# K of the first two tiles projected 256 columns wide, and one semaphore and one accumulating output DMA per block of 512 tokens

## Chip, cores, metric

One core of one Trainium2 chip. The metric is the device time of one execution in microseconds (us); the other cores are idle. For every run the record also holds the span of that execution, from the first to the last instruction, and the mean granted TensorE clock (0.999 or 1.000 in all runs told here). The difference of time and span, "time less span", I also call the fixed part. (Spans are recorded to 0.1 us, so a single difference carries up to 0.05 us of rounding.)

## The reference

A layer norm of x (2048 tokens of 640), then two branches added to x: attention of 32 heads of 20 over 8 keys at distance 0, 2, ... 14, and a gated linear unit of width 1536.

```python
x  = A_x                                  # [1, 2048, 640], bf16
xn = (x - mean(x)) / sqrt(var(x) + 1e-5)
q, k, v = split(xn @ wqkv)                # 32 heads of 20
logits = einsum("bhsd,bhswd->bhsw", q, k[pos - 2 * w]) * 20 ** -0.5   # w = 0..7, masked where pos - 2w < 0
o   = einsum("bhsw,bhswd->bhsd", softmax(logits), v[pos - 2 * w])
out = x + o @ wo + ((xn @ w_gate) * (xn @ w_up)) @ w_down
```

## The kernel before

A list of operations is built in program order; a small scheduler derives the semaphores. A DMA has a semaphore of its own and adds 16 to it; whoever depends on the DMA waits for 16.

```python
class Sched:
    def op(self, eng, fn, r=(), w=(), dma=False, name="", group=None):
        # ... dependencies X.deps from the bytes read (r) and written (w)
        if dma:
            X.event = (self.nc.alloc_semaphore(f"dma{self.n_dma}"), 16)
            self.n_dma += 1
    def emit(self, finals):
        # ... per operation: wait_ge for each dependency not known to be met; at the end:
        for X in finals:                       # the output DMAs
            prog["sp"].append((0,) + X.event)
```

The first two tiles of 128 tokens are projected tile by tile, as soon as their normalised rows are there. Five chunks c of the contraction are accumulated; five groups m of 128 output columns lie side by side in the 512-wide fp32 banks of PSUM (four of them in one bank, the fifth in the shared bank bm).

```python
    def proj_tile(which, tiles, bm, at={}):            # its matmul is line L496, 128 x 128
        for c, (t, b) in [(c, tb) for c in range(NCH) for tb in tiles]:
            col = (2 * which + t) * TS
            for m in range(NCH):
                # ... at[c, m]() puts the transposes of later tiles in between
                o = PS[:, b, m * TS:(m + 1) * TS] if m < 4 else PS[:, bm, col:col + TS]
                l, x = wcols(which, c, m), XNT[:, c, t * TS:(t + 1) * TS]
                # ... op("pe", matmul(o, l, x, start=..., stop=...))

    def proj_wide(which, t0, m, b, col):               # tiles 2 and 3: line L503, 128 x 256
        # ... five matmuls, two tiles at once

    bm = 1
    proj_tile(0, [(0, 0)], bm, {(4, 0): lambda: ln_pe(1, 0, 2), (4, 3): lambda: tr(1, 2)})   # Q of tile 0
    part_evac(0, 0, 1, 0, 4, 0, 0)
    proj_tile(0, [(1, 2)], bm)                                                              # Q of tile 1
    part_evac(0, 1, 1, 0, 4, 2, 0)
    ln_apply(3)
    proj_tile(1, [(0, 3), (1, 4)], bm, {(2, 0): lambda: tr(2), (3, 0): lambda: tr(3)})       # K of both
    ln_start(4)
    for t in (0, 1):
        part_evac(1, t, 1, 0, 4, 3 + t, 0)
    # ... then K and Q of tiles 2 and 3 (L503), V of tiles 0 to 3 (L476), the rest
```

The output of three blocks of 512 tokens is computed transposed: five groups of 17 matmuls per block (down_t, L667), each evicted by ScalarE into a slot of DT, turned by a DMA transpose into FACC, and added to the output in DRAM (which holds x by then) by an accumulating DMA from GpSimd. The last block comes untransposed (tail, L697): VectorE adds x from XR and the rows are stored.

```python
    def down_t(j, d):
        # ... 17 matmuls into bank b
        o = DT[:, (NCH * j + d) % 4]
        op("act", lambda e: e.activation(o, PS[:, b, :], ACT.Copy), r=[PS[:, b, :]], w=[o], name=f"fin{j}_{d}")
        f = FACC[j][:, :, cols]
        op("sp", lambda e: e.dma_start_transpose(f, o), r=[o], w=[f], dma=True, name=f"oT{j}_{d}")
        if d < NCH - 1:
            return
        for u in range(0, NJ, 2):
            f2 = FACC[j][:, u:u + 2]
            # ... h = 256 rows of the output
            stores.append(op("pool", ... e.dma_start(h, f2, accum_op=ALU.add), r=[f2, ("out",)], w=[("out", t)], dma=True))
```

## Time and profile before

| | before |
|---|---|
| time, median of the first 3 runs | 253.98 us (253.9 to 254.27) |
| span of the profiled run | 251.6 us (that run: 253.68 us) |
| TensorE busy | 98% of the span |
| chain that ended last | 96% TensorE |
| last wait for a load on the chain | Q weights, landed at 7.18 us |
| last addition on VectorE | starts at 249.33 us |

In the chain's pieces the columns are start, duration, engine and line, and the number of instructions merged. Dividing a piece's duration by its count gives the interval from one matmul to the next, which is what a stream of matmuls costs; the mean duration of one in the grouped view is two to four times as long, since neighbours overlap. The lines themselves stand in the prediction.

### The profile page before, as it was taken

To read this page: it belongs to the slowest core of one execution; us is meant where nothing else is said; L and a number is where in the kernel's file an instruction comes from. 1 tells how busy PE (TensorE), PEld (TensorE's weight loads), DVE (VectorE), ACT (ScalarE), POOL (GpSimd) and SP (SyncE) were. 2 spreads that over 40 slices of the span, in tenths; PEclk is the share of its full clock that TensorE was granted. 3 is DMA by queue.
4 is the path that set the end of the run, shared out by engine and by line. 5 is a ranking of instruction groups with operands and counts; after the bars stand their busy time and mean duration, and the time that the engine had idled before them with its cause. 6 is when DMAs were issued, how large, how long until landed. Compare 5 with 4: busy or idle time off the path is not lost.

```text
span 251.6 us, 3326 instructions
## 1 busy us (share of the span) xinstructions
PE 247.1 (98%) x1299; PEld 129.0 (51%) x1319; DVE 215.8 (86%) x255; ACT 114.6 (46%) x203; POOL 35.9 (14%) x44
## 2 busy tenths in 40 slices
PE   8999999999999999999999999999999999999996
PEld 3995555555544444444444444444444444445775
DVE  5899889999999953999999995999999999993221
ACT  5486657555555557555555554125555011111000
POOL 1000001044433231002331110003000000300300
DMA  6999679657678462355379931495300010581641
GB/s 188 311 263 204 123 204 407 161 105 125 117 135 138 72 125 42 122 215 104 63 130 270 517 95 28 44 341 88 50 3 0 21 42 21 65 125 24 115 115 52
DMA packets 33824, 33.78 MB, mean 134 GB/s; under 512 B 18033, under 2 KB 30321, under 8 KB 33777
## 3 DMA queue, kind: packets, MB, share of 16 engines
q1 hardware_dynamic: 27280, 24.13, 33.5%
q0 software_dynamic: 6240, 9.31, 22.8%
q8 instruction: 10, 0.16, 0.3%
q10 hardware_dynamic: 288, 0.13, 0.2%
q14 instruction: 6, 0.04, 0.1%
HBM read 14.42 MB, written 4.59 MB: 76 GB/s over the span
## 4 chain that ended last, share of the span: by engine, by line
PE 96%; DMA 1%; SPq 1%; issue 1%; DVE 0%
PE PS L642 41%; PE PS L667 22%; PE PS L476 21%; PE PS L697 7%; PE PS L503 2%; PE PS L496 2%; DMA WQKV<-in_A_wqkv_dram 1%; SPq L295 1%; PE PS L435 0%; DVE FOUT L701 0%
## 5 line engine op out<-in xcount | busy, mean ns | idle before, releaser
L642 PE MATMUL PS<-XNT,WU 128*128 128x512 bf16 x237 | 59.0, 379 | 0.2
L642 PE MATMUL PS<-XNT,WG 128*128 128x512 bf16 x232 | 57.9, 379 | 0.4
L476 PE MATMUL PS<-XNT,WQKV 128*128 128x512 bf16 x245 | 53.7, 379 | 0.3
L609 DVE TENSOR_TENSOR PVB<-VO,ATB 128x10240 f16<-128x10240 bf16 x8 | 43.9, 5488 | 0.2
L476 PEld LDWEIGHTS PS<-XNT,WQKV 128*128 128x128 bf16 x250 | 29.4, 118 | 24.4
L644 ACT ACTIVATE USX<-PS 128x512 bf16<-128x512 f32 x48 | 28.7, 597 | 22.6 <-PE PS L642 22.2
L642 PEld LDWEIGHTS PS<-XNT,WU 128*128 128x128 bf16 x240 | 23.5, 98 | 28.3
L642 PEld LDWEIGHTS PS<-XNT,WG 128*128 128x128 bf16 x240 | 23.5, 98 | 28.3
L604 DVE TENSOR_TENSOR PVB<-PVB 128x5120 f16<-128x5120 f16 (+1 forms) x16 | 34.5, 2155 | 0.3
L537 POOL DMA_DIRECT2D LOG<-PE x24 | 21.8, 910 | 55.5 <-DMA LOG<-PE 55.5
L644 ACT ACTIVATE HT<-PS 128x512 bf16<-128x512 f32 x36 | 21.5, 597 | 16.4 <-PE PS L642 16.4
L670 ACT ACTIVATE DT<-PS 128x512 f16<-128x512 f32 x15 | 9.0, 597 | 43.8 <-PE PS L667 40.7
L667 PE MATMUL PS<-HT,WD 128*128 128x512 bf16 x118 | 27.4, 379 | 0.1
L526 DVE TENSOR_TENSOR TMP<-QH,KH 128x2048 f16<-128x2048 bf16 x16 | 19.1, 1216 | 0.7 <-ACT KH L483 0.7
L667 PEld LDWEIGHTS PS<-HT,WD 128*128 128x128 bf16 x120 | 11.8, 98 | 14.1
L526 DVE TENSOR_TENSOR PP<-QH,KH 128x2048 f16<-128x2048 bf16 x16 | 18.9, 1217 | 0.0
L531 DVE TENSOR_TENSOR PP<-PP,TMP 128x4096 f16<-128x4096 f16 x8 | 18.3, 2291 | 0.2
L679 POOL DMA_DIRECT2D out_dram<-FACC x6 | 7.2, 1434 | 79.3 <-DMA FACC<-DT 79.3
L667 PE MATMUL PS<-VO,WO 128*128 128x512 bf16 x74 | 18.4, 379 | 0.0
L701 DVE TENSOR_TENSOR FOUT<-PS,XR 128x320 bf16<-128x320 f32 (+2 forms) x9 | 4.1, 454 | 16.6 <-PE PS L697 16.6
L537 POOL DMA_DIRECT2D PE<-PP x8 | 7.9, 985 | 64.7 <-DVE PP L532 64.7
L483 ACT ACTIVATE VO<-PS 128x512 bf16<-128x512 f32 x20 | 11.9, 596 | 8.6 <-PE PS L476 8.4
(69 smaller groups left out, 231.9 us busy)
## 6 DMA issues: line engine op xcount, KB each, us to landing
PE<-PP POOLq DMA_DIRECT2D x8, 512.0 KB, 4.7
ATB<-LOG SPq DMA_DIRECT2D x8, 512.0 KB, 4.5
LOG<-PE POOLq DMA_DIRECT2D x24, 128.0 KB, 2.7
WG<-in_B_w_gate_dram SPq DMA_DIRECT2D x1, 1920.0 KB, 8.0
WU<-in_B_w_up_dram SPq DMA_DIRECT2D x1, 1920.0 KB, 14.6
WD<-in_B_w_down_dram SPq DMA_DIRECT2D x1, 1920.0 KB, 10.2
out_dram<-in_A_x_dram SPq DMA_DIRECT2D x1, 1920.0 KB, 9.3
out_dram<-FACC POOLq DMA_DIRECT2D x6, 320.0 KB, 5.3
```

The lines of the kernel that those rows point to most:

```text
L476: op("pe", (lambda l, x, c: lambda e: e.matmul(PS[:, b, :], l, x, start=(c == 0), stop=(c == NCH - 1)))(l, x, c), r=[l, x], w=[PS[:, b, :] ...
L483: op("act", lambda e: e.activation(o, PS[:, b, :], ACT.Copy, scale=sc), r=[PS[:, b, :]], w=[o], name=f"pev{which}_{m}_{j}")
L526: return (1.22, lambda: op("dve", lambda e: e.tensor_tensor(o, qw, kw, ALU.mult), r=[q, k], w=[o], name=f"prod{h}_{p}_{c}"))
L531: (2.3, lambda: op("dve", lambda e: e.tensor_tensor(a, a, b, ALU.add), r=[a, b], w=[a], name=f"psum{h}_{p}")),
L537: op("pool", lambda e: e.dma_start(o, i, accum_op=ALU.add), r=[o, i], w=[o], dma=True, name=name)
L604: return lambda: op("dve", lambda e: e.tensor_tensor(o, x, y, ALU.add), r=[x, y], w=[o], name=f"{name}_{b}")
L609: lambda: op("dve", lambda e: e.tensor_tensor(PVB[:], vw, aw, ALU.mult), r=[v, a], w=[PVB[:]], name=f"pv_{b}")),
L642: op("pe", (lambda l, x, c: lambda e: e.matmul(PS[:, b, :], l, x, start=(c == 0), stop=(c == NCH - 1)))(l, x, c), r=[l, x], w=[PS[:, b, :] ...
L644: op("act", lambda e: e.activation(o, PS[:, b, :], ACT.Copy), r=[PS[:, b, :]], w=[o], name=f"guev{which}_{m}_{j}")
L667: op("pe", (lambda l, x, i: lambda e: e.matmul(PS[:, b, :], l, x, start=(i == 0), stop=(i == n - 1)))(l, x, i), r=[l, x], w=[PS[:, b, :]], ...
L670: op("act", lambda e: e.activation(o, PS[:, b, :], ACT.Copy), r=[PS[:, b, :]], w=[o], name=f"fin{j}_{d}")
L697: op("pe", (lambda l, x, i, b, wid: lambda e: e.matmul(PS[:, b, 0:wid], l, x, start=(i == 0), stop=(i == n - 1)))(l, x, i, b, wid), r=[l, ...
```

## The change

Its intent: fewer, wider matmuls at the start (25 of 256 columns for K of tiles 0 and 1 instead of 50 of 128); fewer semaphores, waits and DMAs at the output (five transposes count on one semaphore up to 80, DT has eight slots, one accumulating DMA of 640 KB takes the place of two of 320 KB).

```diff
--- before.py
+++ after.py
@@ -53,6 +53,10 @@
         self.pitch = {}
         self.clock = {e: nc.alloc_semaphore(f"clk_{e}") for e in ("act", "pe", "dve", "pool")}
         self.n_dma = 0
+
+    def dma_event(self, n):
+        self.n_dma += 1
+        return self.nc.alloc_semaphore(f"dma{self.n_dma - 1}"), 16 * n
 
     def sbuf(self, name, shape, dtype, offset):
         t = self.nc.alloc_sbuf_tensor_at(name, shape, dtype, offset=offset)
@@ -90,7 +94,7 @@
                 out.add(g)
         return [(g, q) for g in out for q in quads]
 
-    def op(self, eng, fn, r=(), w=(), dma=False, name="", group=None):
+    def op(self, eng, fn, r=(), w=(), dma=False, name="", group=None, event=None):
         X = _Op()
         X.eng, X.fn, X.name, X.dma = eng, fn, name, dma
         X.needs_tick, X.event, X.pre_know, X.idx = False, None, None, len(self.ops)
@@ -147,8 +151,7 @@
                 before = [] if st is None else st[0] + st[1]
                 self.state[k] = [[X], [], group, before]
         if dma:
-            X.event = (self.nc.alloc_semaphore(f"dma{self.n_dma}"), 16)
-            self.n_dma += 1
+            X.event = event or self.dma_event(1)
         self.ops.append(X)
         return X
 
@@ -272,7 +275,7 @@
     XR = sb("XR", [128, NXR, D])
     NFO = 4
     FOUT = sb("FOUT", [128, NFO, D])
-    DT = sb("DT", [128, 4, JB], FP16, at=K.base[ATB[1].name] + NSB * W * SB * 2)
+    DT = [sb(f"DT{k}", [128, 4, JB], FP16, at=K.base[ATB[k].name] + NSB * W * SB * 2) for k in range(2)]
     FACC = [sb(f"FACC{k}", [128, NJ, D], FP16, at=a) for k, a in
             enumerate((place[0] - NFO * D * 2, K.base[ATB[0].name], K.base[ATB[0].name] + NJ * D * 2))]
     NUS = 7
@@ -483,18 +486,15 @@
         op("act", lambda e: e.activation(o, PS[:, b, :], ACT.Copy, scale=sc), r=[PS[:, b, :]], w=[o],
            name=f"pev{which}_{m}_{j}")
 
-    def proj_tile(which, tiles, bm, at={}):
-        for c, (t, b) in [(c, tb) for c in range(NCH) for tb in tiles]:
-            col = (2 * which + t) * TS
-            for m in range(NCH):
-                if (c, m) in at and t == tiles[0][0]:
-                    at[c, m]()
-                o = PS[:, b, m * TS:(m + 1) * TS] if m < 4 else PS[:, bm, col:col + TS]
-                l, x = wcols(which, c, m), XNT[:, c, t * TS:(t + 1) * TS]
-                st = c == 0 and (m == 0 or m == 4 and t == tiles[0][0])
-                sp = c == NCH - 1 and (m == 3 or m == 4 and t == tiles[-1][0])
-                op("pe", (lambda o, l, x, st, sp: lambda e: e.matmul(o, l, x, start=st, stop=sp))(o, l, x, st, sp),
-                   r=[l, x], w=[o], name=f"pp{which}_{m}_{t}_{c}")
+    def proj_tile(which, t, b, bm, at={}):
+        for c, m in [(c, m) for c in range(NCH) for m in range(NCH)]:
+            if (c, m) in at:
+                at[c, m]()
+            o = PS[:, b, m * TS:(m + 1) * TS] if m < 4 else PS[:, bm, t * TS:(t + 1) * TS]
+            l, x = wcols(which, c, m), XNT[:, c, t * TS:(t + 1) * TS]
+            st, sp = c == 0 and m in (0, 4), c == NCH - 1 and m in (3, 4)
+            op("pe", (lambda o, l, x, st, sp: lambda e: e.matmul(o, l, x, start=st, stop=sp))(o, l, x, st, sp),
+               r=[l, x], w=[o], name=f"pp{which}_{m}_{t}_{c}")
 
     def proj_wide(which, t0, m, b, col):
         o = PS[:, b, col:col + 2 * TS]
@@ -654,6 +654,8 @@
 
     stores = []
 
+    t_event = [None]
+
     def down_t(j, d):
         flush_h(0)
         b = bank()
@@ -666,18 +668,20 @@
                 l, x = WO[:, i - NF, cols], VO[:, i - NF, toks]
             op("pe", (lambda l, x, i: lambda e: e.matmul(PS[:, b, :], l, x, start=(i == 0), stop=(i == n - 1)))(l, x, i),
                r=[l, x], w=[PS[:, b, :]], name=f"dt{j}_{d}_{i}")
-        o = DT[:, (NCH * j + d) % 4]
+        k = NCH * j + d
+        o = DT[k // 4 % 2][:, k % 4]
+        if d == 0:
+            t_event[0] = K.dma_event(NCH)
         op("act", lambda e: e.activation(o, PS[:, b, :], ACT.Copy), r=[PS[:, b, :]], w=[o], name=f"fin{j}_{d}")
         f = FACC[j][:, :, cols]
-        op("sp", lambda e: e.dma_start_transpose(f, o), r=[o], w=[f], dma=True, name=f"oT{j}_{d}")
+        op("sp", lambda e: e.dma_start_transpose(f, o), r=[o], w=[f], dma=True, name=f"oT{j}_{d}",
+           event=t_event[0])
         if d < NCH - 1:
             return
-        for u in range(0, NJ, 2):
-            f2 = FACC[j][:, u:u + 2]
-            t = NJ * j + u
-            h = ohbm[t * TS:(t + 2) * TS, :].rearrange("(u p) n -> p u n", p=TS)
-            stores.append(op("pool", (lambda h, f2: lambda e: e.dma_start(h, f2, accum_op=ALU.add))(h, f2), r=[f2, ("out",)],
-                             w=[("out", t)], dma=True, name=f"oacc{t}"))
+        acc = FACC[j][:]
+        h = ohbm[j * JB:(j + 1) * JB, :].rearrange("(u p) n -> p u n", p=TS)
+        stores.append(op("pool", lambda e: e.dma_start(h, acc, accum_op=ALU.add), r=[acc, ("out",)], w=[("out", j)], dma=True,
+                         name=f"oacc{j}"))
 
     def tail(t, nb):
         j, rows = t // 4, slice((t % 4) * TS, (t % 4 + 1) * TS)
@@ -758,15 +762,23 @@
             t_ln[0] += 1.45
 
     bm = 1
-    proj_tile(0, [(0, 0)], bm, {(4, 0): lambda: ln_pe(1, 0, 2), (4, 3): lambda: tr(1, 2)})
+    proj_tile(0, 0, 0, bm, {(4, 0): lambda: ln_pe(1, 0, 2), (4, 3): lambda: tr(1, 2)})
     part_evac(0, 0, 1, 0, 4, 0, 0)
-    proj_tile(0, [(1, 2)], bm)
+    proj_tile(0, 1, 2, bm)
     part_evac(0, 1, 1, 0, 4, 2, 0)
     ln_apply(3)
-    proj_tile(1, [(0, 3), (1, 4)], bm, {(2, 0): lambda: tr(2), (3, 0): lambda: tr(3)})
+    for c in range(NCH):
+        if c in (2, 3):
+            tr(c)
+        for m in range(NCH):
+            o = PS[:, bm, 2 * TS:] if m == 4 else PS[:, 3 + m // 2, m % 2 * 2 * TS:(m % 2 + 1) * 2 * TS]
+            l, x = wcols(1, c, m), XNT[:, c, 0:2 * TS]
+            st, sp = c == 0 and m % 2 == 0, c == NCH - 1 and m in (1, 3, 4)
+            op("pe", (lambda o, l, x, st, sp: lambda e: e.matmul(o, l, x, start=st, stop=sp))(o, l, x, st, sp),
+               r=[l, x], w=[o], name=f"pw1_{m}_0_{c}")
     ln_start(4)
-    for t in (0, 1):
-        part_evac(1, t, 1, 0, 4, 3 + t, 0)
+    for m in (0, 2):
+        part_evac(1, 0, 2, m, 2, 3 + m // 2, 0)
     ln_pace(12.0)
     for u in (0, 1):
         part_evac(u, 0, 2, 4, 1, bm, 2 * u * TS)
```

## The prediction

> **What bounds the kernel now.** I read the page's first part and its chain of waits, then the chain in order of time for the first 20 us (where the first part of the change lies), then the waits of the last 22 us and the DMA issues (where the second part ends).
>
> ```profile
> PE 247.1 (98%) x1299; PEld 129.0 (51%) x1319; DVE 215.8 (86%) x255; ACT 114.6 (46%) x203; POOL 35.9 (14%) x44
> ...
> PE 96%; DMA 1%; SPq 1%; issue 1%; DVE 0%
> ```
>
> TensorE is busy in 98% of the span and the chain that ended last is 96% TensorE. A busy share alone proves little, as the ends of matmuls are modelled, so I looked for gaps in the chain in order of time:
>
> ```profile
> 3.55 3.63 DMA WQKV<-in_A_wqkv_dram
> 7.18 0.05 issue
> 7.23 0.36 PE PS L496 x3
> 7.59 0.17 PE PS L435 x3
> 7.76 2.73 PE PS L496 x47
> 10.49 0.28 PE PS L435 x5
> 10.77 0.56 PE PS L496 x10
> 11.33 0.28 PE PS L435 x5
> 11.61 1.12 PE PS L496 x20
> 12.73 5.46 PE PS L503 x50
> 18.18 0.05 issue
> ```
>
> The last thing that is waited for on the path is a load of Q weights, landing at 7.18 us. From there to 249.3 us it is one stream of matmuls; the 0.05 us pieces of "issue" come once per about 49 matmuls and fit one record missing from the trace (49 pieces in 10.74 us plus 0.05 is 10.79, which is 50 times 216 ns), so I count them as no gap. The end is then: 7.2 us of start, the sum of the matmul intervals, the last addition on VectorE (249.33 for 0.29 us), and the last store. Only what alters the number or the interval of matmuls, or puts a wait into that stream, can move the time. L496 is the 128-wide projection (100 matmuls, Q and K of tiles 0 and 1), L503 the 256-wide one, L435 the transposes.
>
> The durations of single matmuls would mislead: the grouped view gives 220 ns for one at L496 and 273 ns at L503, but those contain the fill and drain that neighbours share. What counts is the interval, from the chain: 1.12 us / 20 = 56.0 ns, 0.56 / 10 = 56.0 ns, and 5.46 / 50 = 109.2 ns. (The piece of 47 reads 58.1 ns. It holds the start of Q of tile 1, where the issue rate drops for half a microsecond near 8.3 us, close to the end of ScalarE's copy of that tile; that is upstream of the change and stays.)
>
> For the output side, the waits of the last 22 us, then three lines of the waits of the whole span and three of the DMA issues:
>
> ```profile
> DVE FOUT L701 <- PE PS L697: 16.6, 9, 4.2
> POOL out_dram L679 <- DMA FACC<-DT: 14.4, 1, 14.4
> ACT DT L670 <- PE PS L667: 3.1, 1, 3.1
> ```
>
> ```profile
> POOL out_dram L679 <- DMA FACC<-DT: 79.3, 3, 42.8
> ...
> ACT DT L670 <- PE PS L667: 40.7, 14, 3.1
> ...
> ACT DT L670 <- remote: 3.1, 1, 3.1
> ```
>
> ```profile
> out_dram<-FACC POOLq DMA_DIRECT2D x6, 320.0 KB, 5.3
> XR<-in_A_x_dram SPq DMA_DIRECT2D x4, 160.0 KB, 7.7
> FACC<-DT SPq DMA_TRANSPOSE x15, 2.3
> ```
>
> GpSimd's 79 us are idle time of an engine with nothing else to do. The eviction into DT waits for TensorE and never, as far as the view shows, for its buffer: 14 of the 15 waits name TensorE, and the one put down to "remote" is 3.1 us, just as long as the others, so it too is the wait for 17 matmuls. No TensorE wait stands in these views after 7.2 us.
>
> **What the Trainium skill says.** "TensorE: Matmul & The Clock Gate", section "Wait — 56ns, not 53.3ns?", gives the start-to-start of back-to-back warm matmuls as N / 2.4 GHz plus about 2.5 ns: 55.8 ns for 128 and 109.2 ns for 256. The trace agrees to the digit (56.0 and 109.2). The same page, "Back-to-back issue gap", says that a stream of weight loads and matmuls sustains about 81 ns per matmul at N = 128; here the trace differs (56 ns with one weight load of 118 ns per matmul beside it), and the trace decides. That matters: with 81 ns the first part of the change would be worth 50 x 81 - 25 x 109 = 1.3 us. "DMA: Bandwidth & Descriptors", section "Why a DMA increments its semaphore by 16 and not by 1", says that with several DMAs on one semaphore only the full sum tells that all have landed. The change waits for 80 = 5 x 16, so it is sound, but whoever needs one transpose now waits for all five. The same page, "Anatomy of one DMA — SWDGE (gpsimd) path", fits 2.0 us plus bytes / 436 GB/s; that would be 2.75 us for 320 KB, and the trace shows 5.3, so I don't use it.
>
> **Part 1, K of tiles 0 and 1.** Removed: 50 matmuls of 128 columns (two tiles x 5 chunks x 5 column groups) with 50 weight loads. Added: 25 of 256 columns with 25 weight loads. The same columns go through the array, so only the fixed part of each interval is saved: 50 x 56.0 = 2.80 us against 25 x 109.2 = 2.73 us, a gain of 0.07 us (the skill's formula gives 25 x 2.5 ns = 0.06). The 25 weight loads saved are 25 x 118 ns = 2.95 us of the weight-load row, all beside matmuls: at 56 ns per matmul they plainly do not set the pace. All of the 0.07 us lies on the path, provided that no wait appears. Four could:
> - K weights. The five chunks are issued from 4.98 to about 7.3 us and land 3.7 to 4.2 us after issue, so at about 8.7 to 11.1 us. Chunk 0 is first used near 9.4 us, chunk 4 near 12.1. Slack 0.7 to 1 us, and the new order asks for them at most 0.07 us earlier.
> - Transposes of tiles 2 and 3 stay before chunks 2 and 3. VectorE finishes their inputs near 10.1 and 10.8 us; they run at 10.49 and 11.33 and would move up by 0.03 and 0.05 us.
> - The next 256-wide group needs ScalarE's copy of tile 3, over at 12.35 us, and starts near 12.6. The copy follows the transpose, which moves up as well, so the slack shrinks only by what the last ten matmuls save, 0.03 us.
> - Banks. The four K evictions (0.6 us each) become four of the same 512 columns, ready at the same place in the stream (about 0.3 us before its end); the banks are next used by V after 18 us, when they have long been read.
>
> **Part 2, transposes and output.** DT grows from four slots to eight and waits for a slot become waits for a whole block. Slot 0 is reused at the ninth eviction (second block, fourth), some 40 us after block 0's transposes landed: no wait. One 640 KB accumulating DMA replaces two of 320 KB per block, 6 issues become 3. GpSimd spends 2.39 to 2.42 us on a pair; I estimate 1.5 to 2.4 us for one, as the number of rows is the same. Nothing waits for GpSimd. The last block's pair is issued at 234.0 us and has landed by about 243; the program ends at 251.6. The final waits for stores become three fewer, but they stand in front of the wait for the last store (0.8 us), which hides them. Worth on the path: 0.
>
> Sum: 253.98 - 0.07 - 0 = 253.91 us.
>
> **Rivals.**
> (a) A wait takes the place of the saving: chunk 2 or the copy of tile 3 comes too late by a hair. For: slacks of 0.2 us, and in the half microsecond near 8.3 us TensorE did slow down beside such a copy. Against: everything that it waits for moves up too. It would return the 0.07 us, or add up to 0.1: 253.9 to 254.1.
> (b) The bigger output transfer delays the reload of XR for tile 14. For: that load, issued at 236.4 us, took 6.0 us against 2.7 for tile 15's, since it ran beside the two accumulating DMAs, and VectorE's addition for tile 14 starts at 242.41, 0.05 us late by the rhythm of 2.307 us (240.05 + 2.31 = 242.36). Against: if the one DMA starts 1.2 us later because all its descriptors are made first, and ends later by the same, VectorE makes it up in the idle 1.8 us before each following addition; eight banks let TensorE run on. Time unchanged, unless XR comes 7 us late.
> (c) The narrow matmuls are paced by weight loads, as the skill's 81 ns would have it, and halving them gains over a microsecond: 252.7. Against: 56 ns measured in this very stage.
> (d) Fewer semaphores and waits shorten the fixed part outside the span (253.7 of that profiled run against a span of 251.6). I see nothing in the views for it; up to some tenths, 253.6.
>
> **Range and chances.** 2% is 5.1 us; the largest thing I can build from these views is 1.3 us. The three runs before lie 0.37 us apart (253.9 to 254.27), five times the gain, so the width of the range is that of the measurement and of (a) and (d): 253.4 to 254.4. Within 2%: 0.98, 0.01 on either side.
>
> **What would show it.** In the changed profile: no line of 128-wide matmuls for K, 50 matmuls in the 128-wide group instead of 100, a new group of 25 of 256 columns with 109 ns intervals, and the 256-wide group of tiles 2 and 3 beginning 0.07 us earlier against the landing of the Q weights. Output: three issues of 640 KB, evictions still waiting for TensorE alone, XR of tile 14 landing between 5 and 8 us, the last addition and the last store in the same rhythm. I am wrong if a TensorE wait appears between 9 and 13 us or after 230 us, if the interval at 256 columns is not 109 ns there, or if the span falls by more than 0.3 us, which would mean a cost that these views do not show. The start (weights landing at 7.18 us) may vary between runs by more than the gain.

## The result, and the profile after

| | before | after |
|---|---|---|
| median, 6 runs each, same rounds | 254.06 us (253.65 to 254.29) | 253.64 us (253.39 to 254.07) |
| ratio, after over before | | 0.9987, 95% interval 0.9973 to 1.0001 |
| span of the profiled run | 251.6 us | 251.6 us |
| time less span | 2.08 us (27 runs of the later rounds, 2.03 to 2.13) | 1.79 us (6 runs, 1.77 to 1.81) |

A ratio here is the mean time of one kernel's runs over that of the other's of the same rounds, so not quite the ratio of the medians. The change is within 2%: faster by an estimated 0.33 us, with an interval from 0.03 us slower to 0.69 us faster, so that no difference is just not excluded.

The page of the kernel after, first line and summary of the chain:

```profile
PE 248.1 (99%) x1294; PEld 128.7 (51%) x1294; DVE 215.7 (86%) x255; ACT 114.6 (46%) x203; POOL 32.5 (13%) x41
...
PE 96%; DMA 1%; SPq 1%; issue 0%; DVE 0%
```

The bound is the same. TensorE's matmul and weight-load counts now agree (1294 each); in the trace of before 20 matmul records were missing. So the regular 0.05 us pieces of "issue" there were missing records, as the prediction took them to be: here the chain has no such piece after 18 us. Its pieces in order of time, whole from the landing of the Q weights to the end:

```profile
3.55 3.73 DMA WQKV<-in_A_wqkv_dram
7.28 0.05 issue
7.33 0.36 PE PS L496 x3
7.69 0.17 PE PS L438 x3
7.86 1.62 PE PS L496 x27
9.47 1.09 PE PS L777 x10
10.57 0.28 PE PS L438 x5
10.84 0.55 PE PS L777 x5
11.39 0.28 PE PS L438 x5
11.67 1.09 PE PS L777 x10
12.76 5.46 PE PS L503 x50
18.22 53.96 PE PS L479 x250
72.18 77.70 PE PS L642 x360
149.88 18.35 PE PS L669 x85
168.22 25.90 PE PS L642 x120
194.12 36.69 PE PS L669 x170
230.81 18.53 PE PS L701 x153
249.34 0.02 issue
249.37 0.29 DVE FOUT L705
```

L777 is the new group: 1.09 us for ten, 109 ns each. K with the two sets of transposes takes 12.76 - 9.47 = 3.29 us. Before, its first 20 matmuls are the 2.73 us of the piece of 47 less the 1.62 us that the 27 of Q take here, so 1.11; with 0.28, 0.56, 0.28 and 1.12 that makes 3.35 us. The 0.06 us is there. Counted from the landing of the Q weights, as the prediction asked, the 256-wide group of tiles 2 and 3 starts 0.07 us earlier (12.76 - 7.28 = 5.48 us against 12.73 - 7.18 = 5.55). The span does not show it, because the Q weights landed 0.10 us later in this run. From the start of the 256-wide group of tiles 2 and 3 to the last addition both traces read the same: 249.33 - 12.73 = 236.60 us before and 249.37 - 12.76 = 236.61 after. Not one of the changes to the output side moved TensorE's stream.

The output side, after: waits from 229 us to the end, and two lines of the DMA issues of the page and of its window from 230 us.

```profile
POOL out_dram L683 <- DMA FACC<-DT: 17.0, 1, 17.0
DVE FOUT L705 <- PE PS L701: 15.4, 9, 3.0
ACT DT L675 <- PE PS L669: 3.1, 1, 3.1
```

```profile
out_dram<-FACC POOLq DMA_DIRECT2D x3, 640.0 KB, 6.7
```

```profile
out_dram<-FACC POOLq DMA_DIRECT2D x1, 640.0 KB, 6.6
```

The same three waits as before, no new one. GpSimd's timeline, before and then after (start, duration, what, in brackets the idle time ahead of it):

```profile
234.03 2.39 POOL L679 DMA_DIRECT2D out_dram<-FACC  x2 [14.42 <-DMA FACC<-DT]
```

```profile
234.12 1.26 POOL L683 DMA_DIRECT2D out_dram<-FACC  x1 [17.04 <-DMA FACC<-DT]
```

One DMA of twice the size costs GpSimd about as much as one of the two did. The reload of XR for tile 14 took 5.4 us instead of 6.0, and the addition of tile 14 now starts in the rhythm of the others. The reload for tile 15 took 4.1 us instead of 2.7; its addition kept the rhythm too.

So where do some 0.3 us come from, if the span of the profiled run is the same? From the last row of the table: each run of the kernel after has a shorter time outside its span.

### The profile page after: what moved, and what is told of

The parts are those of the page before. It is cut to its first block, busy times and chain, and to the rows that moved or that the text cites. A ratio compares the mean times of both kernels' runs of the same rounds, so it can differ in the third digit from the quotient of the medians.

```text
span 251.6 us, 3277 instructions
## 1 busy us (share of the span) xinstructions
PE 248.1 (99%) x1294; PEld 128.7 (51%) x1294; DVE 215.7 (86%) x255; ACT 114.6 (46%) x203; POOL 32.5 (13%) x41
## 4 chain that ended last, share of the span: by engine, by line
PE 96%; DMA 1%; SPq 1%; issue 0%; DVE 0%
PE PS L642 41%; PE PS L669 22%; PE PS L479 21%; PE PS L701 7%; PE PS L503 2%; DMA WQKV<-in_A_wqkv_dram 1%; PE PS L777 1%; SPq L298 1%; PE PS L496 1%; PE PS L438 0%; DVE FOUT L705 0%
## 5 line engine op out<-in xcount | busy, mean ns | idle before, releaser
L642 PE MATMUL PS<-XNT,WU 128*128 128x512 bf16 x240 | 59.6, 379 | 0.0
L642 PE MATMUL PS<-XNT,WG 128*128 128x512 bf16 x240 | 59.6, 379 | 0.0
L526 DVE TENSOR_TENSOR TMP<-QH,KH 128x2048 f16<-128x2048 bf16 x16 | 19.2, 1219 | 0.0
L526 DVE TENSOR_TENSOR PP<-QH,KH 128x2048 f16<-128x2048 bf16 x16 | 18.9, 1219 | 0.0
L647 DVE TENSOR_TENSOR HT<-HT,USX 128x512 bf16<-128x512 bf16 x36 | 14.4, 418 | 1.7 <-ACT USX L644 1.7
```

The source lines that it names most:

```text
L526: return (1.22, lambda: op("dve", lambda e: e.tensor_tensor(o, qw, kw, ALU.mult), r=[q, k], w=[o], name=f"prod{h}_{p}_{c}"))
L642: op("pe", (lambda l, x, c: lambda e: e.matmul(PS[:, b, :], l, x, start=(c == 0), stop=(c == NCH - 1)))(l, x, c), r=[l, x], w=[PS[:, b, :] ...
L647: h_pending.append(lambda: op("dve", lambda e: e.tensor_tensor(h, h, o, ALU.mult), r=[h, o], w=[h], name=f"h{m}_{j}"))
```

## The experiments

The first four runs keep one part of the change each. Of the columns in the tables, "GpSimd instructions" counts the whole program of that engine as built, waits and branches included. One instruction can hold two waits: as built, 15, 21 and 150 waits added at the end became 8, 11 and 76 instructions.

### Part 1 alone: e1_wideK

```diff
 the kernel before, with proj_tile, the K loop and its two evictions of the kernel after
```

> Part 1 alone (K of tiles 0 and 1 in 25 matmuls of 256). Theory A (the prediction: only the matmul intervals count, 0.07 us on the path, part 2 worth nothing): 0.07 us below the kernel before, so the whole of what the full change gives (ratio 0.9997). Theory B (part 2 shortens something outside TensorE's stream, some 0.25 us, because the measured medians fell by 0.4 us while the profiled span stayed at 251.6): 0.07 us here as well, but then clearly less than the full change; the time outside the span stays at that of before, about 2.0 us.

### Part 2 alone: e2_out

```diff
 the kernel after, with proj_tile(1, [(0, 3), (1, 4)], ...) and the evictions of the kernel before
```

> Part 2 alone (shared semaphore, eight slots, one output DMA per block; K as before). Theory A: 0 us, ratio 1.0000 within 0.0006. Theory B: about 0.25 us below before (ratio 0.9990), and the time less the span about 1.8 us instead of 2.0.

### The two halves of part 2: e2a_sem and e2b_dma

```diff
 e2a_sem: e2_out, but
-        acc = FACC[j][:]
+        for u in range(0, NJ, 2):        # two output DMAs of 320 KB, as before
 e2b_dma: the kernel before, but
-        for u in range(0, NJ, 2):
+        acc = FACC[j][:]                 # one output DMA of 640 KB
```

> Shared semaphore and eight slots only; still two output DMAs of 320 KB per block, so three more DMAs, waits at the end and semaphores than the run with all of part 2. Theory A: 0 us. Theory B, if it is the number of semaphores (12 fewer than before): about 0.2 us; if it is the output DMAs and the final waits: 0 us.

> One output DMA per block only; a semaphore for each transpose and four slots, as before. Theory A: 0 us. Theory B, if it is the number of semaphores (3 fewer): 0.05 us; if it is the output DMAs and final waits: about 0.25 us. In both the one DMA of 640 KB lands 6 to 7 us after its issue, before the program's end by 10 us.

All four ran on one chip with 11 runs of before (median 253.82 us):

| run | median us | ratio to before (95%) | time less span, us | GpSimd instructions |
|---|---|---|---|---|
| before | 253.82 | | 2.08 | 106 |
| e1_wideK | 254.03 | 1.001 (0.9997 to 1.0023) | 2.08 | 106 |
| e2_out | 253.41 | 0.9985 (0.9973 to 0.9997) | 1.81 | 95 |
| e2a_sem | 253.67 | 0.9992 (0.998 to 1.0004) | 1.80 | 101 |
| e2b_dma | 253.62 | 0.9995 (0.9982 to 1.0008) | 1.77 | 100 |

Part 2 alone gives the whole gain, part 1 alone none that shows (its chain has the same K pieces as the kernel after: 1.09, 0.55 and 1.09 us). Theory A, that part 2 is worth nothing, falls. But it is right about the path: even in e2b_dma, whose span came out at 252.0 us, the stretch from the 256-wide group to the last addition is 249.74 - 13.13 = 236.61 us:

```profile
13.13 5.46 PE PS L503 x50
...
249.74 0.29 DVE FOUT L699
```

In e1_wideK, e2_out and e2a_sem it is 236.61 us too. Spans differ from run to run (251.5 to 252.6 us in these rounds) with the first 13 us, where loads, layer norm and transposes take turns. What part 2 changes lies outside the span: 0.27 to 0.31 us, in each of the four kernels with any part of it, and not in e1_wideK. And each half alone gives all of it, which no count of semaphores, DMAs or final waits explains as so much for each one: it looked like a step.

### What the step depends on: x1_spare, x2_pool, x3_odma

Two things had moved in every kernel with a part of part 2: the highest semaphore number in use (224 before; 221 in e2b_dma, 212 in e2a_sem, 209 with both halves), and the number of GpSimd instructions (106; 100, 101, 95). The programs of other engines shrank as well, but not in all of them: ScalarE's from 262 to 254 instructions in e2a_sem, while e2b_dma kept 262; SyncE's from 101 to 99 in e2b_dma, while e2a_sem kept 101.

```diff
 x1_spare: the kernel after, and ahead of all other semaphores
+        self.spare = [nc.alloc_semaphore(f"spare{i}") for i in range(15)]
 x2_pool: the kernel after, and at the end of GpSimd's program
+                if ename == "pool":
+                    prog[ename] += [(0, clock["dve"], 1)] * 21      # waits met since the first us
 x3_odma: the kernel before, and for the six last stores
+            if name.startswith("odma"):
+                X.event = self.odma[0]                              # one semaphore, up to 96
```

> The changed kernel with 15 semaphores reserved ahead of the others and never used: 114 are in use as before, but the highest number in use is 224, that of the kernel before (209 in the changed kernel, 221 in the run with only the output DMA merged, 212 in the run with only the shared semaphore). Theory S1 (the fixed part outside the span depends in a step on the highest semaphore number): time less span 2.08 us, so 0.29 us slower than the changed kernel. Theory S2 (on the count in use) and theory P (on the number of GpSimd instructions): 1.79 us, as the changed kernel.

> The changed kernel with 21 waits on GpSimd that are met already, put at the end of its program; in the program as built it then has 106 GpSimd instructions, as the kernel before (95 in the changed kernel, 101 and 100 in the two halves of part 2). Theory P: time less span 2.08 us. Theories S1 and S2: 1.79 us.

> The kernel before with one semaphore for its six last stores: 124 semaphores in use, highest number 219, instead of 129 and 224; GpSimd has its 106 instructions, SyncE its 101, TensorE its stream. Theories S1 and S2: time less span about 1.79 us, 0.29 us faster than before, with nothing else of the change in it. Theory P: 2.08 us, no gain. If the shared semaphore only takes five waits off the end of the span, at most 0.1 us there.

| run | median us | ratio to before (95%) | time less span, us | highest semaphore | GpSimd instructions |
|---|---|---|---|---|---|
| before, 9 runs | 253.86 | | 2.09 | 224 | 106 |
| x1_spare | 254.06 | 1.0004 (0.999 to 1.0018) | 1.78 | 224 | 95 |
| x2_pool | 254.02 | 1.0005 (0.999 to 1.002) | 2.06 | 209 | 106 |
| x3_odma | 254.33 | 1.0017 (1.0004 to 1.0031) | 2.09 | 219 | 106 |

The semaphore theories fall, both ways: with the high numbers the fixed part stays short, with fewer semaphores it stays long. GpSimd's program decides: 21 waits that wait for nothing, put behind its last DMA some 16 us before the end, bring 0.27 of the 0.29 us back (its four runs scatter more than the others', 1.99 to 2.21 us). (The medians here contain the spans, which scatter by more than the effect; read the fixed part. The whole of the 0.5 us that x3_odma is slower than before lies in its span, 252.1 to 252.3 us in four runs, and its stretch to the last addition is again 236.61 us.)

### A step or a slope, and of which engine: y1_pool103, y2_pool171, y3_sp110, y4_poolmid

```diff
 the kernel after, with waits that are met already:
 y1_pool103: 15 at the end of GpSimd's program
 y2_pool171: 150 at the end of GpSimd's program
 y3_sp110:   21 on SyncE, ahead of its first store of the last block
 y4_poolmid: 21 on GpSimd, ahead of its first output DMA
```

> The changed kernel with 15 waits, already met, at the end of GpSimd's program: 103 GpSimd instructions as built (101 gave 1.80 us outside the span, 106 gave 2.06 and 2.08). Theory P-step (a step somewhere between 101 and 106): 1.79 or 2.08 us, which tells the side of the step; theory P-slope (so much per instruction): about 1.95 us.

> The same with 150 such waits: 171 GpSimd instructions. P-step with one step only: 2.08 us. P-step with a step every so many instructions (some 64): 2.3 to 2.4 us. P-slope, by the 0.29 us for 11 instructions: near 3.8 us.

> The changed kernel with 21 waits, already met, on SyncE, put before its first store of the last block, where it is idle: 110 SyncE instructions as built (99 in the changed kernel, 101 before), GpSimd at 95. If the step belongs to GpSimd alone: 1.79 us. If any short program has it near a hundred instructions: 2.08 us.

> The changed kernel with 21 waits, already met, on GpSimd, ahead of its first output DMA, where it is idle since 150 us, instead of at the end: 106 GpSimd instructions. If the length of the program counts: 2.08 us outside the span. If it is what GpSimd runs at its end: 1.79 us.

| run | median us | ratio to before (95%) | time less span, us | GpSimd instructions |
|---|---|---|---|---|
| before, 7 runs | 254.15 | | 2.08 | 106 |
| y1_pool103 | 253.91 | 0.9993 (0.9978 to 1.0008) | 2.10 | 103 |
| y2_pool171 | 253.63 | 0.9982 (0.9967 to 0.9996) | 1.79 | 171 |
| y3_sp110 | 253.5 | 0.9977 (0.9962 to 0.9992) | 1.80 | 95 |
| y4_poolmid | 253.68 | 0.9982 (0.9965 to 0.9998) | 1.97 | 105 |

(y4_poolmid had 105 instructions as built, not the 106 of its expectation.) From 101 instructions (e2a_sem) to 103 the fixed part goes up by the whole 0.3 us, so P-slope falls. But y2_pool171 refutes every form of P that I had written down: with 171 instructions the fixed part is short again. It is no longer than with 95, so it is not a matter of more work. y4_poolmid met neither of its two expectations: 1.97 us lies between them. y3_sp110 clears SyncE: 11 more instructions there change nothing.

What is shown is that GpSimd's program moves the fixed part; which property of the program does it is not. Lengths of 95, 100, 101 and 171 give 1.77 to 1.81 us, 103 and 106 give 2.06 to 2.11, and 105 with the waits in the middle 1.97. A dependence on where the program ends would not contradict these lengths, but no run tests it. The number of instruction loads within the span, which the DMA view counts in its row "q14 instruction", is not it: 5 packets in the kernel after (1.79 us) and in x2_pool (2.06), 6 in before (2.08) and in y2_pool171 (1.79). Whether the 0.3 us come ahead of the first instruction or after the last can't be told from the records. That stays open.

### A dose for part 1: x5_split

```diff
 the kernel before, in proj (250 matmuls of 512 columns):
-            op("pe", ... matmul(PS[:, b, :], l, x, start=(c == 0), stop=(c == NCH - 1)))
+            for u in (0, 1):                       # two of 256, each with its own weight load
+                o, xu = PS[:, b, u * 256:(u + 1) * 256], x[:, u * 256:(u + 1) * 256]
```

> A dose for part 1, in the other direction: the kernel before with each of its 250 projection matmuls of 512 columns split in two of 256 (and twice the weight loads). If the cost of a narrow matmul is a fixed part of its interval of about 2.6 ns (216 against 2 x 109.2), the time rises by 250 x 2.6 ns = 0.65 us, and the chain shows 500 matmuls 109.2 ns apart. If weight loads of 118 ns set the pace at 256 columns, by 500 x 118 - 250 x 216 = 5 us. If nothing is lost, by 0.

Measured: 254.53 us (254.38 to 255.32) against 253.86, ratio 1.0034 (1.002 to 1.0047). Its chain between 18 and 80 us:

```profile
18.26 54.58 PE PS L479 x500
```

54.58 / 500 = 109.2 ns, against 53.96 us for the 250 whole ones in the kernel after (215.8 ns each): 0.62 us more for 250 splits, 2.5 ns each. The stretch to the last addition grew by the same (237.23 us). So a cut, which adds a matmul and its weight load, costs 2.5 ns on the path, and by that 25 cuts fewer give 0.06 us. Weight loads of 118 ns each do not set the pace of matmuls 109.2 ns apart. The ratio says 0.86 us, with an interval of 0.5 to 1.2, which holds the 0.62.

### A wait that I had not listed

The PE waits of all 14 profiles were read for one at the first matmul of V, right after the 256-wide group. Two have it, both with wide K. x1_spare, a line of the PE waits and one of TensorE's timeline (in brackets the idle time ahead):

```profile
PE PS L480 <- ACT KH L512: 0.7, 1, 0.7
```

```profile
19.16 5.13 PE L480 MATMUL PS<-XNT,WQKV 128*128 128x512 bf16 x23 [0.71 <-ACT KH L512]
```

x2_pool, the same group, 0.3 us:

```profile
18.43 5.78 PE L481 MATMUL PS<-XNT,WQKV 128*128 128x512 bf16 x26 [0.29 <-issue]
```

The view puts one down to the last K eviction, the other to nothing. In the program as built, this matmul waits for two things: ScalarE's eviction of bank 1, over at 14.96 us in x1_spare, and the V weights, 800 KB issued at 9.72 us. So it was the load. The DMA issues of before, x1_spare and x2_pool, in this order (the last figure is the time from issue to landing):

```profile
WQKV<-in_A_wqkv_dram SPq DMA_DIRECT2D x1, 800.0 KB, 7.8
```

```profile
WQKV<-in_A_wqkv_dram SPq DMA_DIRECT2D x1, 800.0 KB, 9.1
```

```profile
WQKV<-in_A_wqkv_dram SPq DMA_DIRECT2D x1, 800.0 KB, 8.4
```

The loads landed at 9.72 + 9.1 = 18.82 us in x1_spare and at 9.72 + 8.4 = 18.12 in x2_pool. The lengths of the two waits, 0.7 and 0.3 us, are not quite what they cost, because the record of V's first matmul is missing. Two lines of x1_spare for the tile WQKV show this (250 weight loads from 18.9 us on, 245 matmuls from 19.2):

```profile
L480 PEld LDWEIGHTS PS<-XNT,WQKV x250: 117/118/125, 18.9 to 72.5; 128*128 128x128 bf16 x125
L480 PE MATMUL PS<-XNT,WQKV x245: 379/379/380, 19.2 to 72.7; 128*128 128x512 bf16 x123
```

The weight loads tell it better: V's first starts at 18.91 us in x1_spare and at 18.18 in x2_pool, 0.1 us after the landing in both. The cost is in the stretch to the last addition, 250.25 - 12.99 = 237.26 us and 249.53 - 12.68 = 236.85 instead of 236.61: 0.65 and 0.24 us. In before, whose load took 7.8 us and landed at 17.53, V's first weight load starts at 17.91; with a like distance it could have started at about 17.6, so some 0.3 us were to spare. In y2_pool171, with 8.3 us, nothing was to spare: it starts at 18.14, again 0.1 us after the landing, and the stretch is 236.62.

By this account a faster start is worth nothing beyond that margin, which changes from run to run. x1_spare also shows the first of the four waits that I had listed, a chunk of K weights that landed late, at 10.01 us, on its chain:

```profile
5.44 4.56 DMA WQKV<-in_A_wqkv_dram
10.01 0.05 issue
10.05 0.74 PE PS L778 x5
```

No run altered these loads, so what the margin does to the mean time is not shown. Nor do the spans tell: 35 runs with wide K have a mean span of 251.89 us, 47 with narrow K 251.86 (standard errors 0.05 and 0.04, over different rounds and kernels). The difference of 0.03 us has an error of 0.06, as large as the gain that was due.

## Why the prediction was right, and where not

The time (253.64 us in a range of 253.4 to 254.4, predicted 253.9) held. The range was made wide for the scatter of the runs and for rivals (a) and (d); the sum itself left out the larger part of the gain.

- **The bound.** Right: 236.60 and 236.61 us of one stream before and after; the 0.05 us pieces were missing records.
- **Part 1, 0.07 us.** The term was right in size: 3.35 to 3.29 us in the chain, and 2.5 ns per cut by the dose. Rival (c), pacing by weight loads, is refuted by the same dose. As a gain in the time it does not show, neither in e1_wideK nor in the spans; the scatter there is larger than 0.06 us.
- **The four waits that could appear.** None of the four did in the profile of the kernel after; the first did in one of the later runs (x1_spare, 0.3 us or so). But the list lacked the nearest one, the V weights.
- **Part 2, worth 0 on the path.** Right for the path in every profile of it. Wrong in the estimate of GpSimd's issue (1.5 to 2.4 us; it was 1.26 to 1.29), which had put the cost down to rows; it goes with the number of DMAs.
- **Rival (b), XR.** It did not happen; XR of tile 14 came 0.6 us sooner.
- **Rival (d), the fixed part.** This is the failed term: the sum gave it 0, with "I see nothing in the views for it", and it is 0.29 us, four times the gain that was counted. The rival allowed it "up to some tenths", which covers it, but its reason, fewer semaphores and waits, fails: with five semaphores fewer than before x3_odma stays long, with three fewer e2b_dma is short, and with 76 more instructions of waits than the kernel after y2_pool171 is short. What moves it is GpSimd's program (x2_pool, y1_pool103: waits added, nothing else), and not in a way that grows with its length (y2_pool171); by which property is open. The two spans and times at hand before could not have shown this: it takes a second kernel to see that 2.08 us is not a constant.

The sum as it should have been: 0.06 from the matmuls, at most, and 0.29 from outside the span, 0.35 us. The ratio gives 0.33; with its interval of -0.03 to 0.69 us, that the two are so close is luck.

## What to carry to other kernels

Where one engine's stream is the path and its intervals are known to a nanosecond, the worth of widening matmuls can be counted: here 2.5 ns for each one saved together with its weight load. For gains of tenths of a microsecond, take the time less the span of every run as a quantity of its own; it can tell in four runs what the times leave in their scatter, and shows whether an "improvement" is in the kernel at all. Before counting on a faster start, look at the next load that its stream runs into, including the ones on which no wait shows yet.

## What the Trainium skill lacked or had wrong

- "TensorE: Matmul & The Clock Gate", "Back-to-back issue gap", gives some 81 ns per matmul at 128 columns and 131 ns at 512 in a stream with weight loads. Here such a stream ran at 56.0 ns for 128, 109.2 for 256 and 215.8 for 512 (53.96 us / 250), each with its own weight load; the formula that the page calls that of an isolated matmul fits all three.
- "DMA: Bandwidth & Descriptors", "Anatomy of one DMA — SWDGE (gpsimd) path": 2.0 us plus bytes / 436 GB/s would be, as an estimate, 3.5 us for 640 KB and 2.75 for 320; the accumulating DMA of 640 KB to DRAM took 6.6 to 6.7 us, those of 320 KB, issued in pairs, 5.3 in the median.
- The same section calls descriptor generation small and variable and gives no figure for it; here the profile has GpSimd busy for 1.26 to 1.29 us on an accumulating DMA of 640 KB and for 1.17 to 1.70 on one of 320 KB (spans of GpSimd in a profile are rough).
- "Runtime: NRT & Kernel Launch", "The ~15µs preamble/postamble breakdown", lists fixed stages. No page that I read has it that the time outside the instructions depends on GpSimd's program: 1.77 to 1.81 us at 95, 100, 101 and 171 instructions, 2.06 to 2.11 at 103 and 106.
